# First attention scores as pieces of the strip schedule of a fused attention and MLP kernel

## The chip, the cores and the metric

The kernel runs on one core of a Trainium2 chip. The core has a matrix engine (TensorE, PE in the profile; its weight loads are PEld), a vector engine (VectorE, DVE), a scalar engine (ScalarE, ACT), a general engine (GpSimd, POOL) and an engine that only issues transfers and handles semaphores (SyncE, SP). Each engine runs its own instructions in the order in which they were written, and waits on semaphores for the others. Matmuls write into eight banks of PSUM of 128 x 512 float32, numbered 0 to 7.

The metric is the device time of one execution in microseconds, as the median of several runs. Of the kernel before three runs are shown: 1035.71 us in the median, 1033.7 the lowest and 1037.14 the highest.

## The reference

2048 tokens of width 448 go through two branches, and a gate mixes them:

```
g = sigmoid((x * gate_w).sum(-1))
qkv = x @ wqkv                       # 16 heads of width 28
a = softmax(q @ k^T * 28**-0.5) @ v  # per head, then a @ wo
b = gelu(layernorm(x) @ w1 + b1) @ w2 + b2   # inner width 1792
out = g * a + (1 - g) * b
```

All of it is float32. The kernel keeps that accuracy on a matrix unit that takes a rounded format (float32r in the code) by splitting operands into a rounded high part and the rest, the low part; a product is then the sum of high*high, high*low and low*high.

## The kernel before

**Stages.** First the projections to queries and keys (class QK), then values and gate (Val), then the MLP (Up: 14 pieces for each of four chunks of 512 tokens; Down: four tiles of 128 tokens for each chunk), then attention in turns. Queries, keys, values and the MLP result (`gbs`) go through DRAM tensors.

**Strips.** All stages up to the MLP have a contraction that is cut into four strips of 32 partitions. A matmul of one strip uses a quarter of the rows of the matrix unit, so matmuls of four strips run at once. The class `Strips` is a planner that runs in Python while the program is written: it keeps a clock for each strip, and at each step gives the strip that is free first its next matmul. A piece is worked off one strip after another and accumulates in one PSUM bank out of six; two further banks (6 and 7) take the row maxima. A piece that changes from one strip to the next is handed over by a semaphore increment that SP issues: SP waits for the last matmul of the piece on the old strip, and the first matmul on the new one waits for SP (`end`, `sig = nc.sync.sem_inc(hand, 1)`). When the last strip of a piece is done, `close` writes its eviction: for Down a ScalarE copy out of PSUM and a transfer to `gbs`, which ScalarE issued too. `st.free[bank]` notes when the bank is free by the planner's estimate.

**Row maxima.** Softmax is taken with the true row maximum, which is found by matmuls of its own: 1024 matmuls (class `RowMax`, line 212), each followed by a VectorE reduction (line 214). As many as VectorE can take run among the strips; the rest follow in the turns, up to two per turn (`lone`).

**Turns.** The attention works on 1024 units; a unit is one block of 128 keys against 512 queries for one of four heads that lie on the four strips. Units are numbered so that heads vary fastest. `turn_of` writes the scores of four units, three matmuls each (high keys with high queries, low keys with high queries, high keys with low queries; line 1168), in two halves of two units and two PSUM banks; the maximum comes in as one more row of the contraction (a row of -1 in the keys, the maxima as a row of the queries). `soften` writes the exponentials of a half (ScalarE, line 1174). The first half is one instruction over two banks, the second half is two instructions while row maxima are left. Then `batch` multiplies the exponentials of the four units of the turn before with the values (line 1212). Three pairs of PSUM banks take turns: `pairs` sorts (0, 1), (2, 3), (4, 5) by when the planner thinks both banks are free. Turn 0 had no products to do; in their place stood fillers (`idle`, line 974): full-height matmuls of the keys with themselves whose result nobody reads, four ahead of turn 0 and six behind its scores.

**Entering attention.** When the last Up piece is closed, `early` writes what the first turns need: the queries of chunk 0 and the keys and values of the first four heads. In the kernel before, POOL did nearly all of it: it cleared the tile for the low keys (`la`), fetched queries (`yl`), keys (into `la`) and values (`va`), rounded them into the high parts (`yh`, `ka`), subtracted to get the low parts, fetched the maxima (`load_ms`) into the rows of the queries, and last fetched the row of -1 (`key_row`) into `ka`. At this point the four Down tiles of the last chunk are still to do, and fill TensorE for about 35 us.

Of the kernel before, what the change touches and what calls it, by code (L numbers as in the profile page):

```python
# [15 lines left out]
P = 128  # L16
# [19 lines left out]
def kernel(ctx: ExitStack, tc: tile.TileContext, xt, wqk, wv, wo, xk, w1, b1, w2, b2,  # L36
# [204 lines left out]
    HOP = 0.51  # L241
    RATE = 230.0
# [130 lines left out]
    class Down(Piece):  # L373
# [31 lines left out]
        def close(self, st, now):  # L405
# [6 lines left out]
            st.free[self.bank] = st.act + 0.1  # L412
            nc.scalar.dma_start(gbs[self.c * TPC + self.i], gb)
            st.use("act", now, 0.5)

    class Strips:


        def __init__(self, tiles):
# [5 lines left out]
            self.free = {b: 0.0 for b in range(6)}  # L425
# [9 lines left out]
            self.handed = 0  # L435

# [24 lines left out]
        def pick(self, s, now, over=None):  # L461
            for x in self.live:
# [16 lines left out]
        def run(self):  # L479
            while self.tiles or self.live:  # L480
# [401 lines left out]
    def early(st, now):  # L882
# [9 lines left out]
        st.at(now + 4.0, lambda: nc.gpsimd.memset(la.bitcast(F32), 0.0), pool=2.2)  # L892
# [45 lines left out]
    for b, m in enumerate((0, 3, 4)):  # L938
        x = QK(0, m)
        x.bank = b  # L940
        highs, lows = x.full()
        if b == 0:
            ops = sum((highs[t] + lows[t:t + 1] for t in range(4)), [])
        else:
            ops = sum(highs, []) + lows
        for i, (w, v) in enumerate(ops):
            if b == 0 and i in WARM:
                warm(WARM[i])
            nc.tensor.matmul(bk[:, b], w, v, start=(i == 0), stop=(i == len(ops) - 1), skip_group_check=True)  # L949
        x.close(strips, -2.2 * (2 - b))  # L950
# [20 lines left out]

    def idle(n, b):
        for _ in range(n):
            nc.tensor.matmul(bk[:, b], khi[0][:, 0:P], khi[0][:, 0:CH], start=True, stop=True)  # L974

    idle(4, min(range(6), key=lambda b: strips.free[b]))
# [165 lines left out]
    prob, tail = {}, []  # L1142
# [35 lines left out]
    def turn_of(u, turn):  # L1178
# [11 lines left out]
        ahead = [(u + i) % 4 for i in range(2)]  # L1190
        behind = [(u + i) % 4 for i in range(2, 4)]
        if rowmax.left() and turn not in projected:
            lone(behind, 6, turn)
        for step in range(4):
            for i in range(na):
                if step < 3:
                    score(u + i, step, first + i)
            for i in range(nb):
                if step > 0:
                    score(u + 2 + i, step - 1, second + i)  # L1200
# [92 lines left out]
```

## Time and profile before

| | |
|---|---|
| median of three runs | 1035.71 us |
| lowest and highest | 1033.7, 1037.14 us |
| profiled execution, its own time | 1034.85 us |
| its span, first to last instruction | 1033.1 us |
| around the span | 1.75 us |
| last Up piece leaves TensorE | about 402 us into the span |
| last Down matmul, first filler | 438.22 us |
| first scores of turn 0 | 439.34 us |
| first products (turn 1) | 443.76 us |
| last turn's products | 1016.87 us |

The profiled execution lies 0.86 us under the median of the three runs, inside their spread of 3.4 us. A line such as "439.34 0.51 PE L1168 MATMUL" in the timeline means that an instruction of line 1168 started 439.34 us into the span and that this row of it, which may hold several that overlap, lasted 0.51 us. Matmuls overlap in TensorE, so how long a group takes is read from start to start, not from the durations. In square brackets at the end of a row stands the time for which the engine sat idle before it, and what ended that.

### The profile page before, as it was taken

The page shows a single profiled execution, that of the slowest core. Times are in us where ns is not written, and L with a number is a line of the kernel's source. Part 1 is how long each engine was busy: PE and PEld are TensorE (multiplying, and loading weights), DVE is VectorE, ACT ScalarE, POOL GpSimd, SP SyncE. Part 2 cuts the span into 40 slices and gives each one's busy share as a digit, 9 for nine tenths or more (in the row PEclk, how much of TensorE's full clock was granted, in tenths as well). Part 3 has the DMA queues.
Part 4 walks back from the last instruction along what each step waited for, and adds up shares of the span by engine and source line. Part 5 has one row for each costly group of instructions (what it writes and reads, how often), then busy time and mean ns, then how long its engine had stood idle before and what let it go on. Part 6 is the DMA issues. An engine that isn't in the chain of part 4 may idle for free.

```text
span 1033.1 us, 30973 instructions
## 1 busy us (share of the span) xinstructions
PE 1024.8 (99%) x13170; PEld 676.9 (66%) x13170; DVE 749.2 (73%) x1178; ACT 662.9 (64%) x1018; POOL 372.9 (36%) x396
## 2 busy tenths in 40 slices
PE   9999999999999999999999999999999999999997
PEld 6999999999999999944444444444444444454555
DVE  4899999999999999956666666656666666644101
ACT  5234365034043043089999999999999999959553
POOL 5467569626334036460011001410111223626414
PEclk9999999999999999999999999999999999999999
DMA  7697533221110013251000010310002201121202
GB/s 242 201 264 250 181 109 101 83 65 45 39 38 11 9 42 87 67 145 29 14 18 26 21 36 15 102 34 24 17 27 59 56 12 58 21 73 31 73 29 81
DMA packets 47787, 73.20 MB, mean 71 GB/s; under 512 B 13840, under 2 KB 28816, under 8 KB 46848
## 3 DMA queue, kind: packets, MB, share of 16 engines
q1 hardware_dynamic: 33888, 39.11, 13.5%
q0 software_dynamic: 5120, 16.89, 5.7%
q10 hardware_dynamic: 8640, 15.21, 4.1%
q8 instruction: 103, 1.69, 0.7%
q14 instruction: 36, 0.29, 0.1%
HBM read 51.75 MB, written 19.31 MB: 69 GB/s over the span
## 4 chain that ended last, share of the span: by engine, by line
PE 98%; DMA 1%; DVE 0%; ACT 0%; SPq 0%; issue 0%; ACTq 0%; DVEq 0%
PE bk L503 36%; PE bk L1212 25%; PE bk L1168 17%; PE bk L212 16%; PE bk L1030 2%; PE bk L1032 1%; PE bk L1031 1%; PE bk L949 1%; DMA first<-in_xt 1%; DVE raw L715 0%; PE bk L974 0%; DVE mx L214 0%; ACT gb L410 0%; PE bk L1095 0%; SPq L927 0%
## 5 line engine op out<-in xcount | busy, mean ns | idle before, releaser
L214 DVE TENSOR_REDUCE mx<-bk 128x1 f32<-128x512 f32 x1024 | 683.7, 689 | 179.6 <-PE bk L212 155.0
L1174 ACT ACTIVATE p<-bk 128x1024 f32<-128x1024 f32 x745 | 510.9, 758 | 63.7 <-PE bk L1168 37.7
L212 PE MATMUL bk<-kd,qd 28*128 28x512 f32 x1024 | 436.1, 427 | 0.7 <-DVE mx L214 0.6
L212 PEld LDWEIGHTS bk<-kd,qd 28*128 28x128 f32 x1024 | 186.1, 182 | 199.5 <-DVE mx L214 176.7
L503 PE MATMUL bk<-yh,w1f 32*128 32x512 f32 x1568 | 186.4, 391 | 0.0
L503 PE MATMUL bk<-yl,w1f 32*128 32x512 f32 x784 | 161.8, 390 | 0.0
L503 PEld LDWEIGHTS bk<-yh,w1f 32*128 32x128 f32 x1568 | 151.1, 183 | 0.7 <-ACT gb L410 0.2
L503 PE MATMUL bk<-w2h,hh 32*128 32x448 f32 x896 | 143.7, 365 | 0.0
L503 PE MATMUL bk<-w2l,hh 32*128 32x448 f32 x896 | 142.5, 363 | 0.0
L1070 POOL TENSOR_TENSOR ot<-ob,rc 128x512 f32<-128x512 f32 x12 | 15.4, 1286 | 348.0 <-DMA rc<-rls 289.4
L1212 PE MATMUL bk<-p,vb 128*32 128x512 f32 x1024 | 136.6, 605 | 0.0
L1212 PE MATMUL bk<-p,va 128*32 128x512 f32 x1024 | 136.4, 605 | 0.0
L367 POOL TENSOR_TENSOR hl<-h,hh 128x512 fp32r<-128x512 f32 x56 | 72.6, 1308 | 124.4 <-PE bk L503 48.3
L503 PEld LDWEIGHTS bk<-yl,w1f 32*128 32x128 f32 x784 | 104.0, 183 | 0.0
L503 PEld LDWEIGHTS bk<-w2h,hh 32*128 32x128 f32 x896 | 103.4, 183 | 0.3
L503 PEld LDWEIGHTS bk<-w2l,hh 32*128 32x128 f32 x896 | 102.9, 183 | 0.1
L1168 PE MATMUL bk<-yh,ka 29*128 29x512 f32 x512 | 93.2, 470 | 0.1
L503 PE MATMUL bk<-w2h,hl 32*128 32x448 f32 x896 | 88.8, 362 | 0.0
L1168 PE MATMUL bk<-yh,kb 29*128 29x512 f32 x512 | 88.1, 477 | 0.0
L359 ACT ACTIVATE h<-bk,b1s 128x512 f32<-128x512 f32 x56 | 38.3, 683 | 67.9 <-PE bk L503 56.9
L1168 PE MATMUL bk<-yh,la 28*128 28x512 f32 x512 | 80.3, 393 | 0.0
L1168 PE MATMUL bk<-yl,ka 28*128 28x512 f32 x512 | 79.7, 390 | 0.0
(141 smaller groups left out, 1554.1 us busy)
## 6 DMA issues: line engine op xcount, KB each, us to landing
qk<-qo ACTq DMA_DIRECT2D x28, 256.0 KB
raw<-in_xt SPq DMA_DIRECT2D x17, 256.0 KB
vs<-vt ACTq DMA_DIRECT2D x16, 256.0 KB
rc<-rls SPq DMA_DIRECT2D x60, 64.0 KB
bxr<-in_xk POOLq DMA_DIRECT2D x8, 448.0 KB, 6.0
acc<-gbs SPq DMA_DIRECT2D x16, 224.0 KB
out_y<-acc SPq DMA_DIRECT2D x16, 224.0 KB
qd<-qk SPq DMA_DIRECT2D x60, 56.0 KB
```

Of the source, the lines that this page charges most:

```text
L212: nc.tensor.matmul(ps, self.qd[n % 2][r, i * P:(i + 1) * P], self.kd[r, k * 512:(k + 1) * 512], start=True, stop=True)
L214: nc.vector.reduce_max(self.mx[n % 2][:, j, i, k:k + 1], ps, axis=AX)
L359: nc.scalar.activation(h, bk[:, self.bank], AF.Gelu_apprx_tanh, bias=b1s[:, f:f + 1])
L367: nc.gpsimd.tensor_sub(hl[f], h, hh[f].bitcast(F32))
L503: mm = nc.tensor.matmul(bk[:, x.bank, :n], a, b, start=x.first, stop=(len(x.rem) == 1 and m == len(ops) - 1), skip_group_check=True)
L949: nc.tensor.matmul(bk[:, b], w, v, start=(i == 0), stop=(i == len(ops) - 1), skip_group_check=True)
L1030: nc.tensor.matmul(po, h, woh[:, g], start=(g == 0), stop=False, skip_group_check=True)
L1031: nc.tensor.matmul(po, h, wol[:, g], start=False, stop=False, skip_group_check=True)
L1070: nc.gpsimd.tensor_mul(ot[g][:, c * CH:(c + 1) * CH], ob, rc)
L1168: nc.tensor.matmul(bk[:, b], w[r, ks], q[r], start=(p == 0), stop=(p == 2), skip_group_check=True)
L1174: nc.scalar.activation(t[:, i:e], bk[:, b + i:b + e], AF.Exp, scale=SCALE)
L1212: nc.tensor.matmul(bk[32 * j:32 * j + 32, 7], vg[n // NC][:, k, 32 * j:32 * j + 32], prob[4 * b + j], start=(k == 0), stop=(k == NT - 1), ...
```

## The change

Seven things are altered.

- The scores of units 0 to 3 are no longer turn 0. They are pieces (`Unit`) of the strip schedule, each on one strip alone, and are placed by the planner once all Down tiles have begun and 16 us have gone by since the last Up piece (`SCORED`). Their exponentials are written at their `close`, one instruction for each unit, into the space of the second value tile (`vb`), which is loaded only later.
- The turns begin with unit 4, and the first turn already has products to do.
- Both groups of fillers are gone.
- `early` has the queries, keys, maxima and values fetched by SP, beginning 0.6 us after the last Up piece by the planner's clock; the row of -1 is put into the low-key tile before the rounding, so that it comes into the high keys by the rounding itself.
- The rounding into high parts is done by ScalarE (`high`), the subtraction stays on POOL. POOL's clearing of `la` now stands ahead of the low part of the last Up piece.
- The results of the last chunk's Down tiles are sent to `gbs` by SP, not by ScalarE.
- The six banks of the strips are numbered in another order (`BANKS`); and in a turn right after a projection the two halves of a turn change places when the strips of the second half are behind in row maxima.

How the instructions stand now is shown at three places, in the order of the engine concerned (nothing of it is a time).

TensorE where the strips end and the turns begin: `w2h`, `hl` are the last operands of the last Down tiles, `kd`, `qd` those of a row maximum, `yh`, `yl` the queries in their high and low parts, `ka`, `la` the keys, `va` the values, `p` exponentials. Before:

```order
L503 MATMUL bk<-w2h_3761,hl_2960 128x448
L503 MATMUL bk<-w2h_3803,hl_2961 128x448 x2
L974 MATMUL bk<-ka 128x512 x4
L1168 MATMUL bk<-yh,ka 128x512 x2
L1168 MATMUL bk<-yh,la 128x512 x2
L1168 MATMUL bk<-yh,ka 128x512 x2
L1168 MATMUL bk<-yl,ka 128x512 x2
L1168 MATMUL bk<-yh,la 128x512 x2
L1168 MATMUL bk<-yl,ka 128x512 x2
L974 MATMUL bk<-ka 128x512 x6
L212 MATMUL bk<-kd,qd_153 128x512
L1168 MATMUL bk<-yh,ka 128x512 x2
```

Now:

```order
L544 MATMUL bk<-w2h_3761,hl_2960 128x448
L544 MATMUL bk<-w2h_3803,hl_2961 128x448
L1218 MATMUL bk<-yh,ka 128x512 x2
L1218 MATMUL bk<-yh,la 128x512 x2
L1218 MATMUL bk<-yh,ka 128x512 x2
L1218 MATMUL bk<-yl,ka 128x512 x2
L1218 MATMUL bk<-yh,la 128x512 x2
L1218 MATMUL bk<-yl,ka 128x512 x2
L1264 MATMUL bk<-vb,va 32x512 x4
L212 MATMUL bk<-kd,qd_153 128x512
L1218 MATMUL bk<-yh,ka 128x512 x2
```

Both fillers are gone; the first twelve scores behind the strips are now those of units 4 to 7, and the four products of units 0 to 3, whose exponentials lie in `vb`, follow them at once.

TensorE where the first units stand among the Down tiles. Before:

```order
L503 MATMUL bk<-w2h_3737,hl_2959 128x448
L503 MATMUL bk<-w2h_3803,hl_2961 128x448
L503 MATMUL bk<-w2h_3171,hh_2934 128x448
L503 MATMUL bk<-w2h_3761,hl_2960 128x448
L503 MATMUL bk<-w2l_3172,hh_2934 128x448
L503 MATMUL bk<-w2h_3803,hl_2961 128x448
L212 MATMUL bk<-kd,qd_152 128x512
```

Now:

```order
L544 MATMUL bk<-w2h_3171,hh_2934 128x448
L544 MATMUL bk<-w2l_3260,hh_2936 128x448
L544 MATMUL bk<-yh,ka 128x512
L544 MATMUL bk<-w2h_3761,hl_2960 128x448
L544 MATMUL bk<-w2l_3172,hh_2934 128x448
L544 MATMUL bk<-w2h_3291,hh_2937 128x448
L544 MATMUL bk<-yh,la 128x512
L544 MATMUL bk<-w2h_3803,hl_2961 128x448
L544 MATMUL bk<-w2h_3213,hh_2935 128x448
L544 MATMUL bk<-w2l_3292,hh_2937 128x448
L212 MATMUL bk<-kd,qd_152 128x512
L544 MATMUL bk<-yl,ka 128x512
```

A unit takes three slots of its strip between the matmuls of Down tiles on the other three. From the first of these scores to the end of the strips TensorE has 374 matmuls. Of row maxima the strips hold 570 where they held 569, and the turns 454 where they held 455.

SP between the last stored maxima of the MLP stage (`ms_79`) and the fetches of the first turns (`acc<-in_wo` is the output weight). Before:

```order
L233 DMA ms_79<-mt_159 4x32x32
L196 DMA qd_153<-qk 28x512 x2
L196 DMA qd_152<-qk 28x512
L998 DMA acc<-in_wo 128x448
L865 DMA yl<-qk 28x512 x2
```

Now:

```order
L233 DMA ms_79<-mt_159 4x32x32
L196 DMA qd_153<-qk 28x512
L906 DMA yl<-qk 28x512 x4
L196 DMA qd_153<-qk 28x512
L939 DMA la<-ones 4x2048
L889 DMA la<-qk 28x2048 x4
L915 DMA yh<-ms_72 4x512
L901 DMA va<-vs 128x8x128 x2
L416 DMA gbs<-gb 128x448 x2
L416 DMA gbs<-h 128x448 x2
L196 DMA qd_152<-qk 28x512
L1048 DMA acc<-in_wo 128x448
```

Sixteen transfers have come into SP's queue. SP's handovers between strips have no row in this order; in the program as built two of them stand between the second and the third fetch of keys, two between the fourth and the fetch of the maxima, and eight behind the values. At the turns that follow, the rows of TensorE read alike but for the place of one row maximum.

The diff, cut to what acts:

```diff
+    SCORED = 16.0
+    BANKS = (2, 1, 4, 0, 3, 5)
 ...
             nc.scalar.activation(gb, bk[:, self.bank, :D], AF.Copy)
             st.use("act", now + 0.2, 0.56)
             st.free[self.bank] = st.act + 0.1
+            if self.c == NC - 1:
+                nc.sync.dma_start(gbs[self.c * TPC + self.i], gb)
+                return
             nc.scalar.dma_start(gbs[self.c * TPC + self.i], gb)
 ...
+    class Unit(Piece):
+        cost = 0.235
+        def __init__(self, j):
+            super().__init__(0, j)
+            self.rem = {j}
+        def start(self, st, now):
+            return st.scored <= now
+        def ops(self, s):
+            r, top = slice(32 * s, 32 * s + DH), slice(32 * s, 32 * s + DH + 1)
+            h, l, q, ql_ = khi[0], klo[0], qh[0], ql[0]
+            return [(h[top, 0:P], q[top]), (l[r, 0:P], q[r]), (h[r, 0:P], ql_[r])]
+        def close(self, st, now):
+            t = vg[1][:, 4 * self.i:4 * self.i + 4].rearrange("p t d -> p (t d)")
+            nc.scalar.activation(t, bk[:, self.bank], AF.Exp, scale=SCALE)
+            prob[self.i] = t
 ...
-            self.free = {b: 0.0 for b in range(6)}
+            self.free = {b: 0.0 for b in BANKS}
 ...
         def pick(self, s, now, over=None):
+            if over is None and not self.tiles:
+                x = next((x for x in self.units if x.next(s) and x.start(self, now)), None)
+                b = min(self.free, key=lambda b: self.free[b], default=None)
+                if x is not None and b is not None and self.free[b] <= now:
+                    ...
+                    return x
 ...
-        st.at(now + 4.0, lambda: nc.gpsimd.memset(la.bitcast(F32), 0.0), pool=2.2)
+        loads[0] = nc.sync
+        st.scored = now + SCORED
+        st.at(now + 0.3, lambda: nc.gpsimd.memset(la.bitcast(F32), 0.0), pool=1.9)
         for j in range(4):
-            st.at(now + 3.5 + 1.5 * j, lambda j=j: fetch_qq(0, j))
-            st.at(now + 6.5 + 1.5 * j, lambda j=j: fetch_kk(0, j))
-            st.at(now + 14.5 + 2.0 * j, lambda j=j: split_kk(0, j), pool=1.9)
-        st.at(now + 12.0, lambda: split_qq(0), pool=1.9)
-        st.at(now + 10.0, lambda: load_v(0, slice(0, 8)))
-        st.at(now + 11.5, lambda: load_v(0, slice(8, 16)))
-        st.at(now + 16.0, lambda: load_ms(0))
-        st.at(now + 23.0, lambda: key_row(0))
-        st.at(now + 23.5, lambda: nc.gpsimd.memset(lb.bitcast(F32), 0.0), pool=2.2)
+            st.at(now + 0.6 + 0.6 * j, lambda j=j: fetch_qq(0, j))
+            st.at(now + 3.5 + 0.6 * j, lambda j=j: fetch_kk(0, j))
+        st.at(now + 3.2, lambda: loads[0].dma_start(la[DH:P:32].bitcast(F32), ones))
+        def high(h, l):
+            nc.scalar.activation(h, l.bitcast(F32), AF.Copy)
+            st.use("act", st.clock, 0.65)
+            def low():
+                nc.gpsimd.tensor_sub(l, l.bitcast(F32), h.bitcast(F32))
+                st.use("pool", st.clock, 1.35)
+            st.at(st.act + 0.1, low)
+        st.at(now + 7.0, lambda: high(qh[0], ql[0]))
+        for i in range(4):
+            sl = slice(i * CH, (i + 1) * CH)
+            st.at(now + 10.5 + 1.4 * i, lambda sl=sl: high(ka[:, sl], la[:, sl]))
+        st.at(now + 10.6, lambda: load_ms(0))
+        st.at(now + 11.5, lambda: load_v(0, slice(0, 8)))
+        st.at(now + 13.0, lambda: load_v(0, slice(8, 16)))
+        st.at(now + 19.0, lambda: nc.gpsimd.memset(lb.bitcast(F32), 0.0), pool=2.2)
 ...
-    idle(4, min(range(6), key=lambda b: strips.free[b]))
 ...
+        order = list(range(size))
+        if turn in projected and size == 4 and sum(rowmax.cnt[s] for s in behind) < sum(rowmax.cnt[s] for s in ahead):
+            ahead, behind, order = behind, ahead, [2, 3, 0, 1]
 ...
-    u = b = turn = 0
+    u, b, turn = 4, 0, 0
+    begins.add(0)
+    begun(0, 0)
 ...
-        if turn == 0:
-            idle(6, 7)
```

More of the change, by code (lines that the diff above doesn't have):

```diff
@@ L435, in __init__ @@
             self.handed = 0
+            self.units, self.scored = [Unit(j) for j in range(4)], 1e9
         def use(self, engine, start, cost):
@@ L479, in run @@
         def run(self):
-            while self.tiles or self.live:
+            while self.tiles or self.live or self.units:
                 s = min(range(4), key=lambda s: (self.t[s], s))
```

33 lines of the change are left out of this document (18 added, 15 removed).

## The prediction

> **What bounds the kernel now.** I read the page first: who is busy, and the chain of work that ended last.
>
> ```profile
> span 1033.1 us, 30973 instructions
> ...
> PE 1024.8 (99%) x13170; PEld 676.9 (66%) x13170; DVE 749.2 (73%) x1178; ACT 662.9 (64%) x1018; POOL 372.9 (36%) x396
> ...
> PE 98%; DMA 1%; DVE 0%; ACT 0%; SPq 0%; issue 0%; ACTq 0%; DVEq 0%
> ```
>
> The chain is TensorE in 98% of the span. So a microsecond counts only if TensorE has one less of work or waiting. Next I read the place that the change touches, on the timeline of TensorE.
>
> ```profile
> 437.73 0.56 PE L503 MATMUL bk<-w2h,hl 32*128 32x448 f32 x3
> 438.22 1.19 PE L974 MATMUL bk<-ka 128*128 128x512 f32 x4
> 439.34 0.51 PE L1168 MATMUL bk<-yh,ka 29*128 29x512 f32 x3
> ...
> 441.04 1.66 PE L974 MATMUL bk<-ka 128*128 128x512 f32 x6
> 442.63 0.49 PE L212 MATMUL bk<-kd,qd 28*128 28x512 f32 x1
> ...
> 443.76 1.06 PE L1212 MATMUL bk<-p,va 128*32 128x512 f32 x8
> ...
> 445.88 0.64 PE L1212 MATMUL bk<-p,va 128*32 128x512 f32 x4
> ```
>
> The strips end at 438.22. Then come four fillers (1.12 us from start to start), the scores of turn 0 (1.70), six fillers (1.59), turn 1 and its products at 443.76, and the products of units 4 to 7 at 445.88. TensorE is never bare there, yet 2.71 us are fillers, and turn 0 is slow. How fast a turn's scores can go is seen late in the span, where turns hold no row maximum.
>
> ```profile
> 975.37 1.07 PE L1212 MATMUL bk<-p,vb 128*32 128x512 f32 x8
> 976.37 0.51 PE L1168 MATMUL bk<-yh,kb 29*128 29x512 f32 x4
> ...
> 977.27 1.06 PE L1212 MATMUL bk<-p,vb 128*32 128x512 f32 x8
> ```
>
> Products take 1.00 us (975.37 to 976.37), twelve scores 0.90 (976.37 to 977.27). Turn 0 took 0.80 more than that. The reason stands on the waits and on ScalarE's timeline.
>
> ```profile
> PEld bk L1168 <- ACT gb L410: 0.9, 2, 0.5
> ```
> ```profile
> 437.60 0.54 ACT L410 ACTIVATE h<-bk 128x448 f32<-128x448 f32 x1 [32.67 <-PE bk L503]
> 438.55 0.54 ACT L410 ACTIVATE gb<-bk 128x448 f32<-128x448 f32 x1 [0.40 <-PE bk L503]
> 439.55 0.54 ACT L410 ACTIVATE gb<-bk 128x448 f32<-128x448 f32 x1 [0.46 <-ACT gb L410]
> 440.55 0.55 ACT L410 ACTIVATE h<-bk 128x448 f32<-128x448 f32 x1 [0.46 <-PE bk L1168]
> 441.51 6.26 ACT L1174 ACTIVATE p<-bk 128x1024 f32<-128x1024 f32 x9 [0.41 <-PE bk L1168]
> ...
> 989.59 1.02 ACT L1174 ACTIVATE p<-bk 128x1024 f32<-128x1024 f32 x1 [0.20 <-PE bk L1168]
> ```
>
> Before each of the four evictions of the last Down tiles ScalarE had something else to do or to wait for, one per microsecond, and turn 0 waited 0.9 us for two of the banks. Ahead of them ScalarE sat idle for 32.67 us: that is the room into which the change puts its rounding. The nine exponentials behind them, three turns, follow each other without a gap: 6.26 / 3 = 2.09 us a turn. One over two banks takes 1.02 us. The last view is busy time by stage.
>
> ```profile
> 400.00:438.20 38.20, 38.20 (x685) 36.84 (x678) 37.40 (x63) 4.51 (x7) 22.97 (x27) 1.00 0.34 83
> 443.76:902.10 458.34, 458.34 (x4729) 189.40 (x4727) 305.97 (x467) 430.46 (x646) 87.78 (x88) 1.00 0.14 37
> ```
>
> The columns are TensorE, weight loads, VectorE, ScalarE, POOL, each with its count, then the granted clock. In the strips TensorE starts 685 matmuls in 38.20 us, 17.9 a microsecond: in a stage that keeps four strips full a matmul costs 0.056 us. In the turns ScalarE is busy 430.46 of 458.34 us (94%) and TensorE always: a turn is 2.12 us (443.76 to 445.88), set by TensorE, with ScalarE close behind.
>
> **The change, part by part.** I follow the products of units 4 to 7, which were at 445.88, since from there on the order of TensorE reads alike.
>
> *Units in the strips.* Twelve unit matmuls and one more row maximum: 13 x 0.056 = 0.73 us. The strips end at 438.22 + 0.73 = 438.95. The price is this low only while every strip has work; a unit's matmul alone would cost at most what a score costs in a turn, 0.90 / 12 = 0.075, so 12 of them 0.90 us at the upper end.
>
> *Turn 0 and the fillers.* Behind the strips stand twelve scores (0.90), four products (1.00), then a row maximum, twelve scores, a row maximum (2.12 - 1.00 = 1.12), and then the products of units 4 to 7. Without waits these begin at 438.95 + 0.90 + 1.00 + 1.12 = 441.97. They were at 445.88: 3.91 us less.
>
> *Waits that come in.* The order of `BANKS` makes the two banks without a Down tile one pair, so the first half of the scores need not wait. The second half takes the banks of the first two evictions. By the order the first Down tile is done 16 matmuls (0.9 us) before the end, the others 6, 4 and 0 before. ScalarE began 437.60 as the first tile was done; without transfers to issue, four evictions go at 0.57 (0.54 and a small gap). The first then starts about 438.2, the second ends about 439.35, and the second half, which TensorE reaches 0.23 us (a quarter of the 0.90) behind 438.95, waits 0.15 to 0.2 us. The fourth ends about 440.5, and the first exponential, over two banks (1.02 us), ends about 441.5. The second half of the next turn needs its banks at 440.85 (the end of the products without waits) + 0.2 + 0.34 (a row maximum and a quarter of the scores) = 441.4 at the earliest: 0.2 us more with the semaphore's way. Together 0.4. Bounds: nothing, when ScalarE is a little earlier than I think, and 0.9, the wait for evictions in the row above.
>
> *Keys by SP.* The units wait for keys, queries and maxima, and a unit's matmul that waits holds all four strips, since TensorE works in order. POOL's timeline shows what the chain cost before.
>
> ```profile
> 401.31 1.29 POOL L367 TENSOR_TENSOR hl<-h,hh 128x512 fp32r<-128x512 f32 x1 [0.90 <-ACT hh L360]
> 405.32 1.83 POOL L892 MEMSET la<- 128x2048 f32 x1
> ...
> 418.76 0.61 POOL L853 CAST ka<-la 128x512 fp32r<-128x512 f32 x1 [2.45 <-DMA la<-qk]
> 419.45 1.30 POOL L854 TENSOR_TENSOR la<-la,ka 128x512 fp32r<-128x512 f32 x1
> ```
> ```profile
> L848 SPq DMA_DIRECT2D lb<-qk x8: 307/384/410, 442.6 to 794.0; - x8
> L848 POOL DMA_DIRECT2D la<-qk x4: 504/504/509, 407.6 to 411.0; - x4
> ...
> DMA to landing us min/median/max: 3.5/5.5/7.6
> ```
>
> Now the clearing stands directly behind the operation of 401.31, so 402.6 to 404.4. SP issues the row of -1 and four fetches behind it at 0.31 to 0.41 us each, 2.05 at most; two handovers lie among them, for which I leave 1.5 us: the last fetch is out by 408, and landed between 411.5 and 415.6 (3.5 to 7.6 later). ScalarE rounds the first block (0.6, the cast's time), POOL subtracts (1.30): ready between 413.4 and 417.5. The first unit stands 374 matmuls before the end of the strips, 374 / 17.9 = 20.9 us before 438.95: 418.05. So the keys arrive 0.5 to 4.6 us before they are needed; I take no wait. The rounding, five times 0.6, lies in ScalarE's 32.67 us; if that cover were gone it would cost TensorE at most the 3.0 us. POOL loses work. Here the Trainium skill speaks against a gain in the transfers themselves: its page "DMA: Bandwidth & Descriptors", section "Issuing engines are not separate DMA queues", says that transfers of all issuing engines run on the same 16 engines and that another issuer saves only the issuing. By that rule the landing times stay in the range just used, and the sum is the same.
>
> *Handovers on SP.* SP also hands pieces from strip to strip.
>
> ```profile
> SPq L544 <- PE bk L503: 31.0, 12, 8.5
> ```
>
> Twelve times between 390 and 440 it waited for TensorE to do so, 31.0 us in all, so it is mostly idle; an increment behind a fetch is late by at most that fetch. Two of the fetches of keys stand between handovers, 0.31 to 0.41 us each; the planner leaves 0.51 us between a handover and its use, so I take nothing, and 0.8 as the upper end. The last four transfers to `gbs` stand behind all handovers.
>
> *Elsewhere.* One row maximum moves between late turns: at most 2.12 - 1.90 = 0.2 us (975.37 to 977.27 is a turn with none), either way. The swapped halves after projections change no count: nothing.
>
> Sum: 3.91 - 0.4 = 3.5 us less. The profiled execution took 1034.85 us, 1033.1 of it span, so it would be 1031.35; against the median of the three runs, 1035.71, this is **1032.2 us**.
>
> **The rivals.** *ScalarE sets the pace of the first turns.* For it: nine exponentials without a gap and 94% busy. It began the exponentials of units 4 to 7 at 441.51 + 2.09 = 443.60; now it can at 440.5, when its evictions are done, 3.1 us sooner. If TensorE is held to that and never gets it back, 1035.71 - 3.1 = 1032.6. Against it: a turn is 2.12 for TensorE and 2.09 for ScalarE.
>
> *SP's queue delays the strips.* Each of the four handovers among the fetches 0.35 late, 1.4 in all: 3.5 - 1.4 = 2.1 less, 1033.6. For it: nine transfers and four handovers share SP in some six microseconds. Against: the 31.0 us for which SP only waited for such handovers; a queue that waits for TensorE does not make TensorE wait.
>
> *Keys come too late, the slower side.* The first unit holds all strips until its keys are there. It decides when they come more than 0.5 us after the latest time above, and the kernel is slower when it holds TensorE longer than 3.5 us, at landing 11.6 us behind the last issue; with 5 us of waiting 1035.71 + 1.5 = 1037.2. For it: two value fetches of 512 KB follow at once, as they did when one fetch took 7.6. Against: the values are now behind all keys, not between them. The granted clock, 1.00 in both rows above, is the other thing a long wait could cost: the Trainium skill, "TensorE: Matmul & The Clock Gate", section "HAM oscillation — how this bites in real kernels", has the clock halved after gaps of more than about 3.4 us; no run here shows such a gap.
>
> *No net gain.* The strips were not full at their end, or later turns give the time back by transfers that now stand behind others on SP: the median stays at 1035.7. For it: SP's fetches for turn 1 now wait for the last eviction. Against: their data is needed fifteen turns later.
>
> **How the numbers follow.** Forecast 0.52; ScalarE's pace 0.23; SP's queue 0.13; no net gain 0.06; keys late 0.06. A measurement of this kernel tells 0.3%, 3.1 us, from no change. The forecast's own range is 3.9 to 3.0 less, 1031.8 to 1032.7, and with the runs' scatter (-2.0 and +1.4 about the median) three quarters of it are faster by more than 3.1; of ScalarE's case, which lies on the bound, half: 0.39 + 0.11 = 0.5. Slower by over 0.3% is most of the case of late keys: 0.05. The rest, 0.45, is within. The range for 8 in 10 runs from the forecast with all waits gone and the lowest run's scatter, 1035.71 - 3.9 - 2.0 = 1029.8, to the case of SP's queue with the highest's, 1033.6 + 1.4 = 1035.0.
>
> **What would show it.** Right: no row of fillers; strips ending near 438.95; products of units 0 to 3 near 440, those of units 4 to 7 at 442.4 or so; evictions 0.57 apart; four single exponentials at 418 to 430 in ScalarE's former gap; turns of 2.12 us as before. Wrong: a wait of TensorE's weight loads at line 544 for ScalarE, POOL or a transfer near 418 (keys); for SP between 406 and 410 (handovers); exponentials without gaps while TensorE waits for them over many turns (ScalarE's pace); turns longer than 2.12 (gain given back).

## The result and the profile after

The changed kernel takes 1029.99 us in the median of five runs (1029.68 to 1030.58), against 1034.87 us (1033.7 to 1037.14) for the kernel before in five. The ratio is 0.995, with a 95% interval of 0.9935 to 0.9964: about 4.9 us faster. A second set of five, on another chip, gave 1030.22 against 1035.2 and 0.9952 (0.9938 to 0.9966). The forecast was 1032.2 us, so the direction was right and the gain too small.

The page of the changed kernel, the span and the busy times first, then the chain of work that ended last:

```profile
span 1027.9 us, 30949 instructions
...
PE 1020.8 (99%) x13160; PEld 674.6 (66%) x13160; DVE 747.9 (73%) x1178; ACT 665.9 (65%) x1024; POOL 363.4 (35%) x379
...
PE 97%; DMA 1%; ACT 0%; DVE 0%; issue 0%; SPq 0%; ACTq 0%; DVEq 0%
```

TensorE has 4.0 us less of busy time and still fills the span. The span is 5.2 us shorter. TensorE's timeline at the entry into the turns, in the changed kernel:

```profile
438.10 0.50 PE L544 MATMUL bk<-w2h,hl 32*128 32x448 f32 x2
438.30 0.43 PE L1218 MATMUL bk<-yh,ka 29*128 29x512 f32 x1
...
438.64 0.36 PE L544 MATMUL bk<-w2h,hl 32*128 32x448 f32 x1
...
439.79 1.07 PE L1264 MATMUL bk<-vb,va 128*32 128x512 f32 x8
440.78 0.50 PE L212 MATMUL bk<-kd,qd 28*128 28x512 f32 x1
...
441.91 1.06 PE L1264 MATMUL bk<-p,va 128*32 128x512 f32 x8
```

The first scores of a turn (438.30) start before the last Down matmul (438.64). The first products stand at 439.79, and those of units 4 to 7 at 441.91, 3.97 us earlier than before. No row between them shows an idle time. Now ScalarE in the strips and behind them, again in the changed kernel:

```profile
402.86 0.63 ACT L362 ACTIVATE hh<-h 128x512 fp32r<-128x512 f32 x1
...
412.24 2.19 ACT L942 ACTIVATE ka<-la 128x512 fp32r<-128x512 f32 x4 [6.57 <-DMA la<-qk]
418.98 1.27 ACT L440 ACTIVATE vb<-bk 128x512 f32<-128x512 f32 x2 [4.54 <-PE bk L544]
...
437.72 1.12 ACT L412 ACTIVATE gb<-bk 128x448 f32<-128x448 f32 x2 [8.68 <-PE bk L544]
438.74 0.98 ACT L412 ACTIVATE h<-bk 128x448 f32<-128x448 f32 x2
439.76 6.17 ACT L1224 ACTIVATE p<-bk 128x1024 f32<-128x1024 f32 x9
```

The four evictions take 2.0 us in all (437.72 to 439.72), and nine exponentials follow at once from 439.76. Before, the evictions stood a microsecond apart and the exponentials began at 441.51. The two kernels are at the same point when they leave the last Up tile; the kernel before has there:

```profile
402.77 0.63 ACT L360 ACTIVATE hh<-h 128x512 fp32r<-128x512 f32 x1
```

In kernels that differ only behind it this point still lies anywhere from 401.29 to 404.88, and it carries all that follows with it. So single traces are compared by the **entry** from here on: the time from the start of this rounding to the products of units 4 to 7. It is 445.88 - 402.77 = 43.11 us before and 441.91 - 402.86 = 39.05 after, 4.06 less; the second trace of the changed kernel has 39.07.

The difference of the spans, 5.2 us, is made up of 4.06 at the entry, less 0.09 by which the last Up tile was later; 0.2 in the turns (the last products follow those of units 4 to 7 after 570.99 before, 570.78 after); and 1.0 behind the last store, where the prediction had no term. The views of busy time in halves of a microsecond show that last part, before and after; the last two numbers of a row are the share of the transfer engines and GB/s.

```profile
1029.60:1030.10 0.50, 0.00 (x0) 0.00 (x0) 0.00 (x0) 0.00 (x0) 0.00 (x0) 0.73 0.98 369
1030.10:1030.60 0.50, 0.00 (x0) 0.00 (x0) 0.00 (x0) 0.00 (x0) 0.00 (x0) 0.50 0.03 7
```
```profile
1025.40:1025.90 0.50, 0.00 (x0) 0.00 (x0) 0.00 (x0) 0.00 (x0) 0.00 (x0) 0.97 0.98 369
1025.90:1026.40 0.50, 0.00 (x0) 0.00 (x0) 0.00 (x0) 0.00 (x0) 0.00 (x0) 0.50 0.05 14
```

The last data have landed at about 1030.1 and 1025.9. The spans end at 1033.1 and 1027.9: 3.0 us later before, 2.0 us later after, with no work of any engine in the records.

The times differ by a little less than the spans. Around its span the profiled execution took 1.75 us before and 1.89 after; over the changed kernel's five runs it is 1.95 on average, against 1.73 to 1.85 in the runs of the kernel before. So about 0.2 of the microsecond behind the last store is lost again outside the span.

### The profile page after: what moved, and what is told of

Its sections match the earlier page's. It is cut to its first block, busy times and chain, and to the rows that moved or that the text cites. A ratio compares the mean times of both kernels' runs of the same rounds, so it can differ in the third digit from the quotient of the medians.

```text
span 1027.9 us, 30949 instructions
## 1 busy us (share of the span) xinstructions
PE 1020.8 (99%) x13160; PEld 674.6 (66%) x13160; DVE 747.9 (73%) x1178; ACT 665.9 (65%) x1024; POOL 363.4 (35%) x379
## 4 chain that ended last, share of the span: by engine, by line
PE 97%; DMA 1%; ACT 0%; DVE 0%; issue 0%; SPq 0%; ACTq 0%; DVEq 0%
PE bk L544 35%; PE bk L1264 25%; PE bk L1218 16%; PE bk L212 16%; PE bk L1080 2%; PE bk L1081 1%; PE bk L1082 1%; PE bk L1005 1%; DMA qk<-qo 1%; DMA first<-in_xt 0%; DMA vs<-vt 0%; DVE raw L756 0%; ACT L361 0%; DVE mx L214 0%; ACT qo L301 0%
## 5 line engine op out<-in xcount | busy, mean ns | idle before, releaser
L544 PEld LDWEIGHTS bk<-w2h,hh 32*128 32x128 f32 x896 | 105.7, 183 | 0.3
L544 PEld LDWEIGHTS bk<-w2l,hh 32*128 32x128 f32 x896 | 105.0, 183 | 0.1
L544 PE MATMUL bk<-w2h,hl 32*128 32x448 f32 x896 | 91.0, 362 | 0.0
L544 PEld LDWEIGHTS bk<-w2h,hl 32*128 32x128 f32 x896 | 79.7, 183 | 0.2
```

The lines of the kernel that those rows point to most:

```text
L544: mm = nc.tensor.matmul(bk[:, x.bank, :n], a, b, start=x.first, stop=(len(x.rem) == 1 and m == len(ops) - 1), skip_group_check=True)
```

## The experiments

### Fillers

Ten fillers stood in TensorE's way before, 2.71 us of them. One kernel takes them out of the kernel before, another puts them back into the changed one.

```diff
 # the kernel before
-    idle(4, min(range(6), key=lambda b: strips.free[b]))
...
-        if turn == 0:
-            idle(6, 7)
```

> The kernel before without its ten fillers, nothing else changed. Theory A (the fillers cost TensorE what they take from start to start, 1.12 + 1.59 us): products of units 4 to 7 at 445.88 - 2.71 = 443.2, time 2.7 us under the kernel before. Theory B (the first turns go at the pace of ScalarE, whose four evictions with their transfers end at 441.1; the fillers only cover that): exponentials begin at most 0.4 us sooner, products of units 4 to 7 at 445.3 to 445.6, time 0.3 to 0.6 us under the kernel before.

1037.46 us against 1034.63, ratio 1.0024 (1.0014 to 1.0034): by the ratio 2.5 us **slower** (the medians are 2.8 apart). No theory had this. The reason is in the view by stretches (TensorE, weight loads, VectorE, ScalarE, POOL, granted clock, transfers):

```profile
438.00:440.00 2.00, 1.56 (x20) 0.87 (x12) 1.47 (x3) 1.09 (x2) 0.00 (x0) 1.00 0.31 102
440.00:442.00 2.00, 1.69 (x14) 0.78 (x14) 0.02 (x1) 1.09 (x2) 1.18 (x2) 1.00 0.97 312
442.00:444.00 2.00, 1.31 (x11) 0.87 (x13) 0.67 (x1) 1.71 (x3) 1.92 (x3) 0.68 0.78 270
444.00:446.00 2.00, 2.00 (x17) 0.49 (x11) 0.69 (x1) 2.00 (x4) 0.23 (x1) 0.50 0.77 189
```

Stretches of half a microsecond show when it falls and when it is back:

```profile
442.50:443.00 0.50, 0.18 (x2) 0.00 (x0) 0.17 (x1) 0.50 (x1) 0.50 (x2) 0.71 0.89 280
443.00:443.50 0.50, 0.13 (x4) 0.14 (x4) 0.00 (x0) 0.50 (x2) 0.42 (x2) 0.50 0.96 365
...
449.50:450.00 0.50, 0.50 (x8) 0.00 (x0) 0.18 (x1) 0.50 (x3) 0.50 (x1) 0.97 0.91 155
```

The granted clock goes to 0.50 and comes back 6.82 us later: a share of 0.71 in the half microsecond from 442.50 means that it fell at 442.71, and 0.97 from 449.50 that it rose at 449.53. It is not chance of one execution: the mean clock of the nine runs is 0.995 to 0.998, against 0.998 to 1.0 in the 26 of the kernel before. What led to it, on TensorE's timeline of the same run:

```profile
439.93 0.49 PE L1167 MATMUL bk<-yh,ka 29*128 29x512 f32 x1 [0.44 <-ACT gb L410]
...
440.94 0.49 PE L1167 MATMUL bk<-yh,ka 29*128 29x512 f32 x1 [0.27 <-ACT gb L410]
...
443.37 0.79 PE L1167 MATMUL bk<-yh,ka 29*128 29x512 f32 x2 [0.69 <-ACT p L1173]
```

These are three short waits for ScalarE, 1.4 us of idle time in six, which the fillers had been covering. But only the first two, 0.71 us together, stand ahead of the fall: the third lasts from 442.68 to 443.37 and begins just where the clock falls.

```diff
 # the changed kernel
+    idle(4, min(range(6), key=lambda b: strips.free[b]))
...
+        if turn == 0:
+            idle(6, 7)
```

> The changed kernel with the ten fillers put back at the same two places (four behind the strips, six behind the first turn). Theory A (TensorE sets the pace at the entry of the changed kernel): 2.1 to 2.7 us more, products of units 4 to 7 at 441.91 + 2.1 to 2.7 = 444.0 to 444.6. Theory B (ScalarE sets the pace there): part of the fillers is hidden behind its exponentials, 0.5 to 1.5 us more.

1032.12 us, ratio 0.9977 (0.9968 to 0.9987): some 2.6 us of the gain is gone. The entry is 443.89 - 402.12 = 41.77, 2.72 more than without them, which is what the fillers take:

```profile
438.12 1.21 PE L1030 MATMUL bk<-ka 128*128 128x512 f32 x4
439.26 0.51 PE L1224 MATMUL bk<-yh,ka 29*128 29x512 f32 x4
...
440.18 1.66 PE L1030 MATMUL bk<-ka 128*128 128x512 f32 x6
441.77 1.06 PE L1270 MATMUL bk<-vb,va 128*32 128x512 f32 x8
```

From 438.12 to 439.26 and from 440.18 to 441.77 are 2.73 us. So ten fillers cost all of their time in the changed kernel. In the kernel before it has to be asked what they cost, apart from the clock. Two more kernels take out one group each.

```diff
 # the kernel before, first group kept
-        if turn == 0:
-            idle(6, 7)
```

> The kernel before without the six fillers of turn 0; the four fillers ahead of it stay. Without all ten TensorE was busy 1.56, 1.69 and 1.31 of 2 us in three stretches in a row and the granted clock went to 0.5 for some 6 us. Theory A (the clock follows the busy share over a few microseconds, about 80% over 4 us being the border): TensorE is full until 441.0 and waits about 1 us in all between 441 and 443.5 for the exponentials; two stretches of 2 us at 75 to 80%, just at the border: the clock at 1.0, or below it for at most 3 us; products of units 4 to 7 between 42.6 and 44.0 us behind the last rounding of an Up tile (43.1 before). Theory B (only the first of the waits behind the strips counts): the clock stays at 1.0 and the products come 0.3 to 0.5 us sooner.

```diff
 # the kernel before, second group kept
-    idle(4, min(range(6), key=lambda b: strips.free[b]))
```

> The kernel before without the four fillers ahead of turn 0; the six of turn 0 stay. Theory A (busy share over a few microseconds): two waits of 0.44 and 0.3 us between 438 and 441, then the six fillers: the share falls to 1.6 and 1.7 of 2 us and rises again at once, about 82% over 4 us; the clock stays at 1.0, and since ScalarE's evictions set the pace the products of units 4 to 7 stay where they were, 43.0 to 43.1 us behind the last rounding of an Up tile: no gain. Theory B (the two waits in turn 0 alone take the clock down): a stretch at 0.5 to 0.7 from about 442 on, as without all ten, and the products 1 to 2 us later.

Without the six the entry is 445.27 - 402.24 = 43.03, without the four 446.12 - 402.60 = 43.52, against 43.11 with all. Taking out 1.59 us of fillers bought 0.08, and taking out 1.12 us bought nothing: that entry is 0.41 longer, of which 0.39 stands ahead of the first eviction already (437.82 - 402.60 = 35.22 against 437.60 - 402.77 = 34.83; the runs do not show why). The clock stayed up in both. First the stretches of the kernel without the six, then of the one without the four:

```profile
440.00:442.00 2.00, 1.46 (x12) 0.54 (x8) 0.69 (x1) 1.44 (x2) 1.92 (x3) 1.00 0.89 325
442.00:444.00 2.00, 1.81 (x17) 0.82 (x17) 0.69 (x1) 2.00 (x5) 0.51 (x1) 1.00 0.68 207
```
```profile
438.00:440.00 2.00, 1.57 (x10) 0.65 (x6) 0.90 (x2) 1.14 (x3) 0.55 (x1) 1.00 0.59 150
440.00:442.00 2.00, 1.73 (x11) 1.13 (x11) 0.00 (x0) 1.14 (x3) 1.83 (x4) 1.00 0.88 328
```

Some 0.7 us of idle time in four was borne in each, and the kernel without the four even has the two waits (0.43 and 0.27 us) that stand ahead of the fall in the kernel without fillers. So the waits alone do not decide. One reading fits all three kernels. In the one without fillers the clock changes at 442.71, 449.53 and, behind the last store, 1033.21. These are 6.82 and 583.68 us apart, 2 and 171 times 3.413 us, as if the clock were set anew every 3.41 us. The next rows show that last fall, then the step of 3.41 us that ends with the first fall; then the step with the wait in the kernel without the six, and the two steps with the waits in the one without the four, counted back in the same way from their own last falls (1031.33 and 1029.87):

```profile
1033.00:1033.50 0.50, 0.00 (x0) 0.00 (x0) 0.00 (x0) 0.00 (x0) 0.00 (x0) 0.71 0.55 204
439.30:442.71 3.41, 2.63 (x17) 1.08 (x16) 0.86 (x2) 2.05 (x4) 1.89 (x3) 1.00 0.82 271
```
```profile
440.82:444.23 3.41, 2.72 (x25) 1.15 (x25) 1.35 (x2) 3.12 (x5) 1.61 (x2) 1.00 0.78 248
```
```profile
435.95:439.36 3.41, 2.98 (x45) 2.29 (x37) 2.87 (x5) 1.09 (x2) 0.00 (x0) 1.00 0.55 136
439.36:442.77 3.41, 3.13 (x17) 1.83 (x17) 0.00 (x0) 2.14 (x4) 3.15 (x4) 1.00 0.84 300
```

TensorE was busy for 2.63 of 3.41 us (77%) where the clock fell, and for 2.72 (80%) or more where it did not; without the four the two waits fall into two steps. A border between the two would explain all three kernels, and the 80% of the expectation lies close to it, but three kernels do not show that this is the rule.

### Which part of the change is needed: scores, stores, bank numbers

```diff
 # the changed kernel: the first scores stay a turn, without fillers
-            self.units, self.scored = [Unit(j) for j in range(4)], 1e9
+            self.units, self.scored = [], 1e9
...
-    u, b, turn = 4, 0, 0
-    begins.add(0)
-    begun(0, 0)
+    u = b = turn = 0
```

> The changed kernel with the scores of units 0 to 3 as turn 0 again, so no pieces in the strips; no fillers, everything else as in the change. Theory A (only TensorE's slots count): 12 scores cost 0.90 in a turn and 0.67 among the strips, so 0.2 us more. Theory B (what the pieces bring is that four exponentials go into ScalarE's idle time): the exponentials of units 4 to 7 begin 2.09 us later, at 441.8, and the kernel is 1.8 to 2.3 us slower than the changed one.

1031.04 us, ratio 0.9971 (0.996 to 0.9983), and an entry of 443.60 - 402.44 = 41.16: 2.1 us more. It is the trace that shows this difference; the interval touches that of the changed kernel (up to 0.9964), and the medians are 1.05 apart. TensorE has only 0.2 us more of work here by the prediction's count (twelve matmuls at 0.075 for twelve at 0.056), yet it waits:

```profile
440.51 0.50 PE L1218 MATMUL bk<-yh,ka 29*128 29x512 f32 x2 [0.44 <-ACT p L1224]
```
```profile
439.43 6.05 ACT L1224 ACTIVATE p<-bk 128x1024 f32<-128x1024 f32 x9
```

The exponentials start as early as in the changed kernel (439.43 - 402.44 = 36.99 behind the last rounding), but now two turns of them stand ahead of the products of units 4 to 7, not one. The strips do not end sooner without the units: the last Down matmul starts 438.29 - 402.44 = 35.85 us behind the last rounding, against 438.64 - 402.86 = 35.78 with them.

```diff
 # the changed kernel: the last Down tiles stored by ScalarE
-            if self.c == NC - 1:
-                nc.sync.dma_start(gbs[self.c * TPC + self.i], gb)
-                return
```

> The changed kernel with the last four results sent to DRAM by ScalarE again, not by SyncE. Theory A (ScalarE is not on the path): no difference, below 0.2 us. Theory B (the evictions in front of the first exponentials are on the path): evictions one per microsecond instead of 0.5 to 0.57, the first exponential at 441.2 to 441.6 instead of 439.76, products of units 4 to 7 1.2 to 1.8 us later, and the kernel as much slower.

1031.58 us, ratio 0.9976 (0.9967 to 0.9985), an entry of 445.68 - 404.88 = 40.80: 1.75 more. The four transfers push the evictions apart again and with them the exponentials (ScalarE's timeline, then TensorE's):

```profile
439.78 0.54 ACT L412 ACTIVATE gb<-bk 128x448 f32<-128x448 f32 x1 [8.66 <-PE bk L541]
...
442.74 0.54 ACT L412 ACTIVATE h<-bk 128x448 f32<-128x448 f32 x1 [0.46 <-PE bk L1215]
...
443.68 3.90 ACT L1221 ACTIVATE p<-bk 128x1024 f32<-128x1024 f32 x6 [0.40 <-ACT h L412]
```
```profile
444.76 0.50 PE L1215 MATMUL bk<-yh,ka 29*128 29x512 f32 x2 [0.70 <-ACT p L1221]
```

Four evictions take 3.5 us (439.78 to 443.28), and the first exponential comes 38.80 us behind the last rounding instead of 36.90.

```diff
 # the changed kernel
-    BANKS = (2, 1, 4, 0, 3, 5)
+    BANKS = (0, 1, 2, 3, 4, 5)
```

> The changed kernel with the six strip banks numbered 0 to 5 again. Theory A: no difference. Theory B: the first half of the first turn's scores shares its pairs with the first two evictions (ended about 438.8) and waits for them, and the second half for the third (439.3): first products 0.3 to 0.6 us later than 439.79.

1029.46 us in one run, no slower than the changed kernel, but its last Up tile came 0.95 earlier than in that one's trace. The entry is 441.41 - 401.91 = 39.50, 0.45 more, since the exponentials no longer run through:

```profile
438.94 2.00 ACT L1224 ACTIVATE p<-bk 128x1024 f32<-128x1024 f32 x3 [0.17 <-PE bk L1218]
441.30 4.12 ACT L1224 ACTIVATE p<-bk 128x1024 f32<-128x1024 f32 x6 [0.36 <-PE bk L1218]
```

ScalarE idles for 0.36 us before the fourth. In the view of waits TensorE's weight loads for the scores stand 0.3 us for ScalarE's evictions, which they do not in the changed kernel. That the halves of the first turn get their banks in the wrong order is the expectation's argument for it, not shown by itself; all of it rests on one trace.

### The changed kernel again, and without the swapped halves

> The changed kernel again, unaltered, to see what of its gain lies behind the last store. From the issue of the last store to the end of the span there were 4.5 us before and 3.5 after, with the same work. If that microsecond is chance of one execution, this profile may show any value between, and the times lie 3.9 to 5.2 us under the kernel before. If it belongs to the change, it shows 3.5 again and the ratio stays near 0.995.

Its time stands above; entry 39.07, last products 570.81 us later. The end of the span lies 3.4 us behind the issue of the last store again, so this microsecond belongs to the change.

```diff
 # the changed kernel
-        if turn in projected and size == 4 and sum(rowmax.cnt[s] for s in behind) < sum(rowmax.cnt[s] for s in ahead):
-            ahead, behind, order = behind, ahead, [2, 3, 0, 1]
```

> The changed kernel without the exchange of the halves after projections. Both theories: no difference at the entry (products of units 4 to 7 at 441.9). From there to the last products there were 570.99 us before and 570.78 after; if the exchange makes that 0.2 it goes back to 571.0, if not it stays at 570.8.

Entry 39.07, unchanged. From the products of units 4 to 7 to the last products it takes 571.06. Over the other traces this length is 570.46 to 570.94 with the swap and 570.79 to 570.99 without it, where the clock was up. So the swap is worth at most a quarter of a microsecond, and one trace does not show that much. The 1028.67 us of this run come from its last Up tile, 1.57 earlier.

### Who fetches, and the end of the span

```diff
 # the changed kernel: GpSimd fetches
-        loads[0] = nc.sync
         st.scored = now + SCORED
```

> The changed kernel with queries, keys, maxima and values fetched by GpSimd, as before, at the new places in its order. By the durations of its issues (0.5 us each) the last fetch of keys goes out about 410.3 instead of 407.4; rounded and subtracted they are ready at 416 to 420, and the first unit stands at 418. If a piece that waits holds all four strips, TensorE stands still for up to 2 us near 418 and the kernel is that much slower; if the keys land as fast as by SyncE, no difference.

1030.45 us in one run, the span 1028.7. The entry is 441.66 - 401.93 = 39.73, 0.68 more, through a single wait; it is not for keys:

```profile
PEld bk L544 <- POOL hl L369: 0.7, 1, 0.7
```

GpSimd issued two fetches ahead of the low part of the last Up tile, and the strips waited for that. For keys there is no wait at all, though they come from GpSimd's queue. And the end is back at 1024.2 to 1028.7: 4.5 us from the issue of the last store, against 3.5. The same exchange in the kernel before:

```diff
 # the kernel before: SyncE fetches
+        loads[0] = nc.sync
```

> The kernel before, with one line added: the first turn's queries, keys, maxima and values are issued by SyncE instead of GpSimd. Everything else stays, the rounding on GpSimd too. It tells where the last microsecond of the span comes from. Between the issue of the last store and the end of the span lie 4.5 us in the kernel before and in the changed kernel with GpSimd's fetches, and 3.5 us in the changed kernel. Theory A (the end of the span depends on what GpSimd or its program holds, not on the turns): 3.4 to 3.5 us here, the entry into the turns as in the kernel before (products of units 4 to 7 about 43.1 us behind the last rounding of an Up tile), time 0.7 to 1.2 us below the kernel before of the same chip. Theory B (the two kernels' ends differ by chance or by something else of the change): 4.5 us, no gain.

The end is 3.8 us (last store issued at 1029.0, span 1032.8), 0.7 shorter, so the exchange alone does most of it. The whole gained nothing, 1034.56 us against 1034.56, since the entry is 446.43 - 402.79 = 43.64, 0.5 longer: here the strips wait for SyncE's queue.

```profile
PEld bk L503 <- SPq L544: 0.5, 1, 0.5
```

Is it GpSimd's transfers, or only its longer program?

```diff
 # the changed kernel
+        def small():
+            for _ in range(20):
+                nc.gpsimd.memset(lb.bitcast(F32)[0:1, 0:8], 0.0)
+
+        st.at(now + 18.0, small)
```

> The changed kernel with 20 more GpSimd memsets of 8 numbers each in the strips, where GpSimd is idle, and no further transfer by GpSimd. The transfers that fetch instructions are 36 in every run with a long end (4.5 us) and 35 in every run with a short one (3.5 us). Theory A (the length of GpSimd's program: a further block of instructions is fetched and worked off): 36 such transfers and an end of 4.4 to 4.5 us, 1 us slower than the changed kernel, with the same entry into the turns. Theory B (GpSimd's own data transfers lengthen the end, the count of 36 is only their companion): the end stays at 3.5 us.

1028.47 us in one run, its last Up tile 1.27 earlier. The page shows the longer program, and the end of the span shows no effect of it:

```profile
q14 instruction: 36, 0.29, 0.1%
```
```profile
1024.20:1024.70 0.50, 0.00 (x0) 0.00 (x0) 0.00 (x0) 0.00 (x0) 0.00 (x0) 1.00 0.97 366
1024.70:1025.20 0.50, 0.00 (x0) 0.00 (x0) 0.00 (x0) 0.00 (x0) 0.00 (x0) 1.00 0.03 7
```

The data have landed at 1024.7 and the span ends at 1026.7, 2.0 later; from the last issue it is 3.5. The count of instruction transfers was a companion, not the cause. Over all traces the end is 4.4 to 4.5 us in the five kernels where GpSimd issues the first turn's fetches, and 3.4 to 3.8 in the nine traces where SyncE does. The two at 3.8 are the kernel before with SyncE's fetches and the changed kernel with its scores as turn 0, the two of the nine that place no scores among the strips; why is open. What fills the time is not in the records.

## Why the prediction was right or wrong

**The sum of the entry was right, to 0.06 us.** "Without waits these begin at 441.97"; they began at 441.91. Its first step held as a number: the last Down matmul ends at 438.64 + 0.36 = 439.00, where the last of the row of 437.73 had ended at 438.29, so 0.71 later where 0.73 had been added. But that this is the price of the units is not shown, since the strips end no sooner when the scores are a turn again.

**The step that failed is "Waits that come in", 0.4 us.** It measured nothing. It counted the 16 matmuls between the end of the first Down tile and the end of the strips as 0.9 us, and so let the evictions begin at 438.2 and end at 440.5, 0.57 apart. They ran from 437.72, 1.28 us ahead of the strips' end at 439.00, to 439.72, 0.50 apart, so each bank and each exponential was ready when TensorE came. The lower bound of the step, nothing, was the right value.

**A term was missing: 1.0 us at the end of the span.** The sum carried the time behind the last store over as it was, which put this term at nothing; with the 0.4 us above it makes up the difference between the forecast of 3.5 us less and the 4.9 measured. Of SyncE's fetches the prediction counted the landing times, the handovers and GpSimd's relief, all in the strips. That the end of the program depends on who issued them was in no view of the trace before, and the experiments show it without showing why.

**The reasoning under the right sum was only half right.** The prediction took 2.71 us of fillers as time that TensorE gives up for nothing, and "TensorE is never bare" as the sign of its being the bound. The runs without one group of fillers show otherwise: there the time simply turned into waits for ScalarE. What set the entry before was ScalarE, and one rule gives it to within 0.22 us in eleven of the fourteen traces: the first exponential of the turns, plus 2.09 us for each turn of exponentials that stands ahead of the products of units 4 to 7. All times are counted from the last Up rounding.

| kernel | first exponential | turns of exponentials | sum | entry measured |
|---|---|---|---|---|
| before | 38.74 | 2 | 42.92 | 43.11 |
| before, without the six | 38.87 | 2 | 43.05 | 43.03 |
| before, without the four | 39.12 | 2 | 43.30 | 43.52 |
| before, SyncE fetches | 39.26 | 2 | 43.44 | 43.64 |
| after, scores as turn 0 | 36.99 | 2 | 41.17 | 41.16 |
| after, stores by ScalarE | 38.80 | 1 | 40.89 | 40.80 |
| after, GpSimd fetches | 37.60 | 1 | 39.69 | 39.73 |
| after | 36.90 | 1 | 38.99 | 39.05 |
| after, old bank numbers | 37.03 | 1 | 39.12 | 39.50 |
| after, fillers back | 38.16 | 1 | 40.25 | 41.77 |
| before, no fillers | 38.83 | 2 | 43.01 | 45.35 |

The traces without a row (the changed kernel again, without the swap, with the memsets) lie 0.02 to 0.10 us from the rule. The last three rows are the exceptions: exponentials with a gap, fillers that TensorE must work through, and the lowered clock, which cost 2.3 us. So the entry became 4.06 shorter for two reasons on ScalarE: its exponentials begin 1.84 sooner, since it no longer issues transfers between evictions, and one turn of exponentials, 2.09, is done in the strips; together 3.93. On TensorE the removed fillers and the denser scores happen to free the same time, 3.91. In the changed kernel both engines arrive together: no wait of TensorE's, no gap between exponentials. This is why each part is needed and none is worth its own time: fillers back 2.72, scores as a turn 2.1, stores by ScalarE 1.75, old bank numbers 0.45 add up to 7.0, far more than the 4.06.

**The rivals.** ScalarE's pace had the right mechanism for the kernel before, and a price that was off: it let the exponentials of units 4 to 7 begin at 440.5 instead of 443.60; they began at 439.76, which makes 3.8 rather than 3.1. SyncE's queue did not delay the strips of the changed kernel; there is no wait of TensorE for it. The mechanism exists all the same: in the kernel before it cost 0.5 us. Keys were in time: rounding began at 412.24 and the first unit's scores at 418.07, where the prediction had 418.05, and no wait for keys is on record; even issued by GpSimd they held up nothing. Nothing was given back later, since the turns are not longer.

**The clock.** The prediction named it only as the risk of a long wait, and gave the fillers no part in it. By the Trainium skill, "TensorE: Matmul & The Clock Gate", section "HAM oscillation — how this bites in real kernels", gaps of more than about 3.4 us halve the clock. The run without fillers contradicts this as a complete rule: the longest gap in the 3.41 us ahead of the fall was 0.44 us. The Trainium skill says on the same page, section "A second HAM failure mode: psum-queue depth-cycling", that short but frequent idling between groups of matmuls also makes the clock go down and up. With that the trace agrees: 0.50 after waits of 0.44 and 0.27 us. The changed kernel could drop the fillers without this harm: it no longer has the waits that they covered.

**The chances.** A time lower by more than 0.3% was given one half, because the forecast lay 0.4 us beyond that bound. With the wait at nothing the same sum would have been 1031.8, and with the end 1030.8. The remaining 0.8 lies in the kernel before: its median over five runs is 1034.87, not the 1035.71 of three. That the measured time still lies 0.2 us inside the lower end of the range, 1029.8, is luck: 2.0 us of that end were the scatter of the runs, not a cost.

## What to carry to other kernels

A full engine is not always the bound: filler work hides waits, so before counting its removal as gain, look on the other engine for how far its chain reaches, here the first exponential plus 2.09 us for each turn. Filler matmuls may be there for the clock; take them out only together with the waits that they cover, and look at the granted clock in stretches of two microseconds afterwards. When several edits free time on two engines that finish together, price each engine's chain separately and take the longer one, instead of adding up the edits.

## What the runs showed of the hardware

- In the kernel without fillers the granted clock was 0.50 from 442.71 to 449.53, 6.82 us, after idle times of 0.44 and 0.27 us; TensorE had been busy for 2.63 of the 3.41 us ahead of the fall. It stayed at 1.00 in two kernels with some 0.7 us of idle time in four.
- The three changes of the clock in that trace lie 6.82 and 583.68 us apart, 2 and 171 times 3.413 us.
- The time from the issue of the last store to the end of the span depends on which engine issued twelve or so fetches 600 us earlier: 4.4 to 4.5 us with GpSimd, 3.4 to 3.8 with SyncE. Twenty more GpSimd instructions without transfers did not change it. The cause stays open.
- In kernels that differ only behind it, the last Up tile was reached up to 3.6 us apart, at 401.29 and 404.88. The later one is the trace with the stores by ScalarE, the slowest of its ten runs; its clock was 0.50 from 8.09 to 11.50, which by an estimate (half of 3.41 us) explains up to 1.7 of the 3.6. Single traces of these kernels are better compared from a common point inside them than by their totals.
